# mLSTM, top-2 MoE and dense cosine layer on one core: conversions and preparations issued sooner, late weight low halves on VectorE, 128-row gathers for 64-slot tiles

## The chip, the cores and the metric

One Trainium2 chip, one of its cores. The metric is the device time of one execution in microseconds, taken as the median of repeated runs; lower is better.

## What is computed

Three layers follow one another, all in float32. Sizes: batch 2, 8 heads, 768 positions, head size 40, so 1536 tokens of 320 values; 8 experts of 320 x 1024 and 1024 x 320; a dense layer of 320 x 2048 and 2048 x 320.

```python
# 1. mLSTM: a gated recurrence per head, y[t] = sigmoid(o) * (C @ q) / max(|n . q|, 1)
C = f_stab * C + i_stab * outer(v_t, k_t); n = f_stab * n + i_stab * k_t
# 2. mixture of experts, two experts per token
noisy = x @ w_gate + log1p(exp(x @ w_noise)) * noise
top2 of noisy, softmax over the two
out[token] += weight * (relu(x @ w1[e]) @ w2[e])
# 3. dense layer
h = x @ w_in
out = (h * cos(h)) @ w_out
```

The kernel computes the mLSTM in chunks of 128 positions. Matrix products of layers 2 and 3 are made of float32r products of split operands: every operand is written as a high half (a rounded copy) and a low half (the operand minus the copy), and three products, high x high, high x low and low x high, are added.

## The kernel before, in words

The program is one core's, and the order of every engine's instructions is written out by hand. Five queues matter: PE (matmuls), ACT (ScalarE), DVE (VectorE), POOL (GpSimd) and SP (which issues plain DMAs). Each works strictly in the order in which the builder emits, and a function emitted in "step k" stands behind all that was emitted in steps before.

**Steps.** After the attention part come numbered steps k. Steps 0 to 79 are the expert layer: ten groups of eight steps. A group is one expert and a set of token slots; `groups` is: experts 0 and 1 with two slots (128 and 112 rows) for the first batch entry, experts 2 to 7 with four slots (128, 128, 128 and 64 rows) for both entries together, then experts 0 and 1 with two slots for the second entry. So groups 0, 1, 8 and 9 are narrow (240 columns) and groups 2 to 7 wide (448). Step 8g + f does slice f (128 of 1024 hidden values) of group g. From step 79 on the dense layer runs: `moe2_step(k - 79)`, 64 slices: four sets of 384 tokens by 16 slices of 128 hidden values.

**An expert step** (`expert_step`): first `split(k + 2)`, the weights of two steps ahead: ScalarE copies the raw slice (128 x 704) into `wh` (L597), and an engine subtracts to make the low half `wl` (L599), VectorE or POOL by a rule on k; then the first product `mm1` (eight matmuls, L606, into a PSUM tile `pS`); then ScalarE writes `relu` into the high part of `hb` (L658) and VectorE the low part (L661); then `flush`, which emits the second product of the step before (`mm2`, L611, L612, L615, for a fourth slot also L623, L624). The last matmuls of `mm2` (L615) need the low part of `hb`. `wh`, `wl` and three `pS` tiles rotate; at f = 7 the accumulators are copied out and stored (`fin1`).

**Gathers and preparation.** `gather(g, i)` fetches the rows of slot i of group g with an indirect DMA issued by POOL (L558); an index of an unused place is 0, which is a valid row. `prep_slot` transposes them in three matmuls (`prep_x`, L567), ScalarE copies them to `xh` (L569), VectorE makes the low part `xl` and a second part (L570, L572). They are put at steps by hand: those of group 2 at 13, 14, 15 and 15.

**Conversions.** The dense layer's weights come as float64 in 16 slices. `conv_load(f)` loads one, and `conv_ops(f)` gives five operations: three integer operations on VectorE that make a float32 (L726, L729, L733), ScalarE's high half (L736) and VectorE's low half (L739). `conv_sched(f, ks)` puts them at the five steps `ks`, and the load of slice f + 1 at the first of them. Slices 0 to 11 are done from step 18 on, one every 3.75 steps; 12 to 15 at steps written out, between 66 and 92. The results of slices 12 to 15 lie in a weight buffer of the experts.

**A dense slice** (`moe2_step`): `moe2_a`, the first product of 384 columns; `moe2_b`, reduction of the argument (ScalarE L755, VectorE L756, L757); two steps later `moe2_c`, sine and square on ScalarE (L768, L769) and the product with h on VectorE (L770), which frees the `pS` tile; `moe2_d`, the high half on ScalarE (L774) and the low half on POOL or VectorE (L776); and `moe2_e`, the second product. At step 80 the last `mm2` of the experts is flushed between slices 1 and 2.

**Combination.** `comb_gather` (L682) fetches a token's two expert outputs, `comb` (L689 on ScalarE, L691 on VectorE) adds them, `comb_t` prepares them as above. Those of the first 384 tokens stand at steps 66 to 77.

The order of the attention part and of the two routers isn't touched.

Of the kernel before, what the change touches and what calls it, by code (L numbers as in the profile page):

```python
# [9 lines left out]
FT = mybir.dt.float32  # L10
# [31 lines left out]
def tile_mlstm_moe_moe2(ctx, tc, qk, kv, og, gt, wcat, noise, wm1, wm2, cst, out):  # L42
# [304 lines left out]
    def cols(x, n, k):  # L347

        c0 = min(128 * k, DM - 128)
        return x[:n, c0:c0 + 128]  # L350
# [202 lines left out]
    def gather(g, i):  # L553
        d = GX.setdefault(g, {"xg": []})
        _, sz, j = groups[g]
        n = sz[i]
        t = mp.tile([128, DM], FT, name="xgt", tag="xg", bufs=6)
        G.indirect_dma_start(out=t[:n, :], out_offset=None, in_=XD[0:S, :] if g < 2 else XD[:, :],  # L558
                             in_offset=bass.IndirectOffsetOnAxis(ap=(idxe if g < 2 else idx)[:n, j + i:j + i + 1],
                                                                 axis=0))  # L560
        d["xg"].append(t)

    def prep_x(src, np_, xh, xl, n0, ps_=None):
        p = (ps_ or psM)()
        pv = p[:, :3 * np_].rearrange("p (k t) -> p k t", t=np_)
        for k in range(3):
            T.transpose(pv[:, k, :], cols(src, np_, k), ident[:np_, :np_])  # L567
        sl = slice(n0, n0 + np_)
        A.activation(xh[:, :, sl], pv, AF.Copy)  # L569
        V.tensor_tensor(out=xl[:, :, sl], in0=pv[:, 0:2, :], in1=xh[:, 0:2, sl].bitcast(FT), op=OP.subtract)  # L570

        V.tensor_tensor(out=xh[0:64, 2, sl], in0=pv[64:128, 2, :], in1=xh[64:128, 2, sl].bitcast(FT),  # L572
                        op=OP.subtract)
# [11 lines left out]
        prep_x(d["xg"][i], groups[g][1][i], d["xh"], d["xl"], 128 * i, ps_)  # L585

    SP = {}
    POOL_SPLIT = (1, 5, 7, 9, 65, 67, 75)

    def split(k):  # L590
        g, f = divmod(k, 8)
        if g >= NG:
            return
        raw = WB[groups[g][0]]
        wh = mp.tile([128, FW], FR, name="wh", tag="wh", bufs=4)
        wl = mp.tile([128, FW], FR, name="wl", tag="wl", bufs=4)
        A.activation(wh, raw[:, f, :], AF.Copy)  # L597
        eng = V if len(groups[g][1]) == 2 and (k % 2 and k not in POOL_SPLIT or k == 10) else G
        eng.tensor_tensor(out=wl, in0=raw[:, f, :], in1=wh.bitcast(FT), op=OP.subtract)  # L599
        SP[k] = (wh, wl)  # L600

    def mm1(p, n, wh, wl, xh, xl):
        ops = [(wh, 0, xh, 0), (wh, 1, xh, 1), (wl, 0, xh, 0), (wl, 1, xh, 1), (wh, 0, xl, 0), (wh, 1, xl, 1),
# [40 lines left out]
    def flush():  # L644
        if pend:
            pend.pop(0)()

    def expert_step(g, f):
        e, sz, _ = groups[g]
        d = GX[g]  # L650
        n = sum(sz)
        split(8 * g + f + 2)
        wh, wl = SP.pop(8 * g + f)
        p = psS()
        mm1(p, n, wh, wl, d["xh"], d["xl"])
        hb = new_h()
        hh, hl = hb[:, 0:448], hb[:, 512:896]
        A.activation(hh[:, :n], p[:, :n], AF.Relu)  # L658
        for a, z, o in ((0, min(n, 384), 512), (384, n, 448)):
            if a < n:  # L660
                V.scalar_tensor_tensor(out=hb[:, o:o + z - a], in0=p[:, a:z], scalar=0.0,  # L661
                                       in1=hh[:, a:z].bitcast(FT), op0=OP.max, op1=OP.subtract)
        flush()

        def st2():
            if f == 0:
                d["acc"] = [psA() for _ in sz]
            mm2(d["acc"], sz[:3], wh, wl, hh, hl, f == 0, f == 7)
            if len(sz) == 4:
                mm2h(d["acc"][3], wh, wl, hb, f == 0, f == 7)  # L670
            if f == 7:
                fin1(g)
        pend.append(st2)
# [27 lines left out]

    def conv_load(f):
        q = f // 4
        if f % 4 == 0:
            if q < 3:
                W2[q] = wp.tile([128, 2, 4, FW], FR, name=f"w2_{q}")
            else:
                W2[q] = big.tile([128, 2, 4, FW], FR, name="w2q", tag="W")
        raw = wp.tile([128, FW, 2], I32, name="raw2", bufs=2)
        Y.dma_start(raw, wm2[:, f, :].bitcast(I32).rearrange("p (w two) -> p w two", two=2))  # L710
        W2["raw", f] = raw

    def conv_ops(f):
        wh, wl = W2[f // 4][:, 0, f % 4, :], W2[f // 4][:, 1, f % 4, :]
        raw = W2["raw", f]
        lo, hi = raw[:, :, 0], raw[:, :, 1]
        def tmp(name, tag):
            if f < 13:
                return wp.tile([128, FW], I32, name=name, tag="ct", bufs=3)
            return mp.tile([128, FW], I32, name=name, tag=tag, bufs=4)  # L720

        t0 = tmp("c_t0", "wh")
        tt = {}

        def o1():
            V.tensor_scalar(t0, hi, 0x07FFFFFF, 3, op0=OP.bitwise_and, op1=OP.logical_shift_left)  # L726

        def o2():
            V.scalar_tensor_tensor(out=t0, in0=hi, scalar=-0x40000000, in1=t0, op0=OP.bitwise_and, op1=OP.bitwise_or)  # L729

        def o3():
            t1 = tt[0] = tmp("c_t1", "wl")
            V.scalar_tensor_tensor(out=t1, in0=lo, scalar=29, in1=t0, op0=OP.logical_shift_right, op1=OP.bitwise_or)  # L733

        def o4():
            A.activation(wh, tt[0].bitcast(FT), AF.Copy)  # L736

        def o5():
            V.tensor_tensor(out=wl, in0=tt[0].bitcast(FT), in1=wh.bitcast(FT), op=OP.subtract)  # L739
        return [o1, o2, o3, o4, o5]  # L740


# [60 lines left out]
    def moe2_step(k):  # L803
        if k < N2:
            moe2_a(k)
        if 2 <= k:
            moe2_c(k - 2)
        if k < N2:
            moe2_b(k)
        if 2 <= k:  # L810
            moe2_d(k - 2)
        if k < 3 or k in LATE:
            return
        if k < N2:
            moe2_e(k - 3 - sum(k > i for i in LATE))
        elif k == N2 + 1:
            for i in range(N2 - 3 - len(LATE), N2):
                moe2_e(i)
# [161 lines left out]
    put(12, router_a4, 1)  # L980
    for i in range(4):
        put(7 + i // 2, gather, 2, i)
        put((13, 14, 15, 15)[i], prep_slot, 2, i, (psA, psM)[i % 2])
    for g in range(2, NG - 1):
        n = len(groups[g + 1][1])
        for i in range(n):
# [5 lines left out]

    def conv_sched(f, ks):
        if f == 0:
            put(16, conv_load, 0)

        def first():
            o = conv_ops(f)
            o[0]()
            for k, op in zip(ks[1:], o[1:]):  # L1000
                put(k, op)
            if f + 1 < 16:
                put(ks[0], conv_load, f + 1)
        put(ks[0], first)

    K2 = 8 * NG
    for f in range(12):
        k = 18 + (15 * f) // 4
        conv_sched(f, (k, k + 1, k + 2, k + 2, k + 3))
    conv_sched(12, (66, 68, 69, 71, 71))  # L1010
    conv_sched(13, (78, 79, 80, 82, 83))
    conv_sched(14, (83, 84, 85, 88, 88))
    conv_sched(15, (87, 90, 91, 92, 92))
    for c in range(3):
        for k in range(2):
            put((66, 68, 71)[c] + k, comb_gather, 0, c, k)
# [163 lines left out]
```

## Time and profile before

| | us |
|---|---|
| median of 3 runs (lowest, highest) | 506.29 (506.05, 507.14) |
| the profiled execution | 505.76 |
| its span, first to last instruction | 504.0 |
| PE busy | 481.1 |
| VectorE, ScalarE, POOL busy | 353.2, 325.6, 273.1 |

All of these come from the profile page but the first. The span is 1.8 us shorter than the execution that it belongs to. Times in rows are microseconds from the start of the span. In a timeline a row is one instruction or several of one line merged; the number in brackets is the engine's idle time before it, and what ended it. Matmuls are pipelined, so the start of a matmul tells more than its end. TensorE's granted clock was 0.998 in the mean over the span.

### The profile page before, as it was taken

What the parts mean: (1) busy time and instruction counts of PE and PEld (TensorE: products, weight loads), DVE (VectorE), ACT (ScalarE), POOL (GpSimd) and SP (SyncE); (2) the same over time, 40 slices, a digit from 0 to 9 for tenths busy, and PEclk for the clock granted to TensorE, in tenths of its full rate; (3) what the DMA queues carried; (4) which work ended last, traced back from release to release, by engine and by line L of the source; (5) the groups of instructions that cost most, each with busy time, mean ns of one, the idle gap of its engine ahead of it and who ended that gap; (6) DMA issues with size and microseconds to landing.
All of it is one profiled execution on the core that took longest, in us unless ns stands there. A gap on an engine that the chain in (4) does not pass through costs nothing.

```text
span 504.0 us, 9162 instructions
## 1 busy us (share of the span) xinstructions
PE 481.1 (95%) x3295; PEld 466.0 (92%) x3295; DVE 353.2 (70%) x749; ACT 325.6 (65%) x691; POOL 273.1 (54%) x228
## 2 busy tenths in 40 slices
PE   5999889999999999999999989899999999999995
PEld 4998888989999999999999988899999999999995
DVE  4565697874577777787667588589756755787772
ACT  3787856655454545545553765678787787787772
POOL 4654665877558684968587786363364357200000
PEclk9999999999999999999999999999999999999999
DMA  6989754964739274645657373310020012001001
GB/s 200 299 286 295 236 180 144 322 211 152 294 128 322 103 260 176 257 182 188 257 166 263 117 284 100 105 52 1 0 92 29 0 35 84 2 2 39 1 2 45
DMA packets 25429, 74.47 MB, mean 148 GB/s; under 512 B 3840, under 2 KB 11456, under 8 KB 25376
## 3 DMA queue, kind: packets, MB, share of 16 engines
q1 hardware_dynamic: 22784, 65.20, 37.1%
q0 software_dynamic: 2592, 8.61, 5.7%
q8 instruction: 28, 0.46, 0.4%
q14 instruction: 25, 0.20, 0.1%
HBM read 64.57 MB, written 9.22 MB: 146 GB/s over the span
## 4 chain that ended last, share of the span: by engine, by line
PE 79%; DVE 9%; ACT 3%; issue 3%; DMA 2%; POOL 1%; SPq 1%; ACTq 0%; DVEq 0%; POOLq 0%
PE pS L606 34%; PE pA L615 10%; PE pA L611 10%; PE pA L612 10%; PE pS L321 3%; PE pM L567 2%; DMA wraw<-wm 2%; PE pA L262 1%; PE pA L623 1%; PE pA L624 1%; PE pS L317 1%; PE pM L366 1%; PE pA L253 1%; DVE c_t L729 1%; POOL xgt L558 1%
## 5 line engine op out<-in xcount | busy, mean ns | idle before, releaser
L599 POOL TENSOR_TENSOR wl<-wraw,wh 128x704 fp32r<-128x704 f32 x70 | 125.2, 1801 | 59.8 <-ACT wh L597 53.1
L661 DVE SCALAR_TENSOR_TENSOR hb<-pS,hb 128x384 fp32r<-128x384 f32 (+2 forms) x128 | 45.8, 390 | 45.2 <-ACT hb L658 44.5
L597 ACT ACTIVATE wh<-wraw 128x704 fp32r<-128x704 f32 x80 | 62.8, 786 | 15.8 <-PE pA L623 9.3
L606 PE MATMUL pS<-xh,wh 128*128 128x448 f32 (+1 forms) x240 | 69.3, 343 | 0.5 <-ACT xh L569 0.5
L606 PE MATMUL pS<-xh,w 128*128 128x384 f32 x288 | 66.3, 339 | 1.5 <-DVE m_t L770 1.5
L606 PE MATMUL pS<-xh,wl 128*128 128x448 f32 (+1 forms) x240 | 65.9, 329 | 1.0 <-POOL wl L599 1.0
L611 PE MATMUL pA<-wh,hb 128*128 128x320 f32 x208 | 62.3, 309 | 0.0
L612 PE MATMUL pA<-wl,hb 128*128 128x320 f32 x208 | 62.2, 309 | 0.0
L755 ACT ACTIVATE m_t<-pS,magic 128x384 f32<-128x384 f32 x64 | 37.1, 579 | 27.7 <-PE pS L606 27.2
L658 ACT ACTIVATE hb<-pS 128x448 fp32r<-128x448 f32 (+1 forms) x80 | 37.7, 471 | 26.7 <-PE pS L606 19.2
L606 PEld LDWEIGHTS pS<-xh,w 128*128 128x128 f32 x288 | 50.1, 189 | 2.9 <-DVE m_t L770 2.9
L770 DVE SCALAR_TENSOR_TENSOR m_t<-m_t,pS 128x384 f32<-128x384 f32 x64 | 35.4, 553 | 16.9 <-ACT m_t L769 16.3
L615 PE MATMUL pA<-wh,hb 128*128 128x320 f32 x208 | 44.0, 311 | 2.8 <-DVE hb L661 2.6
L606 PEld LDWEIGHTS pS<-xh,wl 128*128 128x128 f32 x240 | 42.8, 189 | 3.6 <-POOL wl L599 1.4
L606 PEld LDWEIGHTS pS<-xh,wh 128*128 128x128 f32 x240 | 40.5, 189 | 1.6 <-ACT xh L569 0.6
L776 POOL TENSOR_TENSOR wl<-m_t,wh 128x384 fp32r<-128x384 f32 x25 | 25.5, 1019 | 30.2 <-ACT wh L774 21.1
L756 DVE TENSOR_SCALAR m_t<-m_t 128x384 f32<-128x384 f32 x64 | 23.1, 361 | 26.4 <-ACT m_t L755 26.2
L606 PE MATMUL pS<-xl,wh 128*128 128x448 f32 (+1 forms) x160 | 39.6, 328 | 0.0
L611 PEld LDWEIGHTS pA<-wh,hb 128*128 128x128 f32 x208 | 38.7, 186 | 0.6
L612 PEld LDWEIGHTS pA<-wl,hb 128*128 128x128 f32 x208 | 38.7, 186 | 0.5
L569 ACT ACTIVATE xh<-pM 128x384 fp32r<-128x384 f32 (+2 forms) x38 | 17.6, 462 | 30.5 <-PE pM L567 30.4
L757 DVE SCALAR_TENSOR_TENSOR m_t<-pS,m_t 128x384 f32<-128x384 f32 x64 | 35.7, 557 | 2.2
(217 smaller groups left out, 1226.7 us busy)
## 6 DMA issues: line engine op xcount, KB each, us to landing
wraw<-wm SPq DMA_DIRECT2D x36, 704.0 KB
raw<-wm SPq DMA_DIRECT2D x16, 704.0 KB
gb<-gd SPq DMA_DIRECT2D x10, 512.0 KB
kv<-kv SPq DMA_DIRECT2D x12, 324.0 KB
qk<-qk SPq DMA_DIRECT2D x24, 160.0 KB
yd<-yt SPq DMA_DIRECT2D x22, 160.0 KB
wraw<-wm SPq DMA_DIRECT2D x8, 352.0 KB
ogt<-og SPq DMA_DIRECT2D x6, 320.0 KB
```

The costliest lines, as they stand in the source:

```text
L597: A.activation(wh, raw[:, f, :], AF.Copy)
L599: eng.tensor_tensor(out=wl, in0=raw[:, f, :], in1=wh.bitcast(FT), op=OP.subtract)
L606: T.matmul(p[:, :n], w[:, 128 * k:128 * k + 128], x[:, m, :], start=(i == 0), stop=(i == 7))
L611: T.matmul(a[:n, :DM], hh[:, s], wh[:, KW:], start=first, stop=False)
L612: T.matmul(a[:n, :DM], hh[:, s], wl[:, KW:], start=False, stop=False)
L615: T.matmul(a[:n, :DM], hl[:, s], wh[:, KW:], start=False, stop=last)
L658: A.activation(hh[:, :n], p[:, :n], AF.Relu)
L661: V.scalar_tensor_tensor(out=hb[:, o:o + z - a], in0=p[:, a:z], scalar=0.0, in1=hh[:, a:z].bitcast(FT), op0=OP.max, op1=OP.subtract)
L755: A.activation(t, m["p"], AF.Identity, bias=magic, scale=0.5 / PI)
L757: V.scalar_tensor_tensor(out=t, in0=m["p"], scalar=0.5 / PI, in1=t, op0=OP.mult, op1=OP.subtract)
L770: V.scalar_tensor_tensor(out=s, in0=s, scalar=1.0, in1=m["p"], op0=OP.subtract, op1=OP.mult)
L776: eng.tensor_tensor(out=m["hl"], in0=m["t"], in1=m["hh"].bitcast(FT), op=OP.subtract)
```

## The change

Seven edits:

- A gather of the fourth slot of a wide group fetches 128 rows instead of 64, and the transposes of a 64-slot tile are made with all 128 rows; the copies out of PSUM still take 64 columns.
- The rule of who makes a weight low half: VectorE for k in 3, 10, 11, 12, 13, 15 and for all k from 66 on, POOL for the rest. Before, VectorE had the odd k of narrow groups but 1, 5, 7, 9, 65, 67 and 75, and k = 10.
- From k = 66 on the low half is emitted after VectorE's low part of `hb` of the same step, not before it.
- Group 2's preparations stand at steps 12, 13, 14, 14.
- Conversions 0 to 11 begin at step 16 instead of 18, in the same rhythm, with the first load at step 14; conversion 12 joins that rhythm (61, 62, 63), its last two operations stay at 71; 13, 14 and 15 are put at other steps.
- The buffer for slices 12 to 15 is taken when it is first written (step 71) and not with the load.
- Slice 0's sine, square and product are emitted at step 80 behind slice 1's reduction, ahead of the flush and of what else stands at that step, instead of at step 81.

```diff
     def gather(g, i):
-        n = sz[i]
+        n = sz[i] if i < 3 else 128
...
     def prep_x(src, np_, xh, xl, n0, ps_=None):
         p = (ps_ or psM)()
-        pv = p[:, :3 * np_].rearrange("p (k t) -> p k t", t=np_)
+        m = 128 if np_ == 64 else np_
+        pv = p[:, :3 * m].rearrange("p (k t) -> p k t", t=m)
         for k in range(3):
-            T.transpose(pv[:, k, :], cols(src, np_, k), ident[:np_, :np_])
+            T.transpose(pv[:, k, :], cols(src, m, k), ident[:m, :m])
+        pv = pv[:, :, :np_]
...
-    POOL_SPLIT = (1, 5, 7, 9, 65, 67, 75)
+    V_SPLIT = (3, 10, 11, 12, 13, 15)
...
         A.activation(wh, raw[:, f, :], AF.Copy)
-        eng = V if len(groups[g][1]) == 2 and (k % 2 and k not in POOL_SPLIT or k == 10) else G
-        eng.tensor_tensor(out=wl, in0=raw[:, f, :], in1=wh.bitcast(FT), op=OP.subtract)
         SP[k] = (wh, wl)
+        eng = V if k in V_SPLIT or k >= 66 else G
+
+        def low():
+            eng.tensor_tensor(out=wl, in0=raw[:, f, :], in1=wh.bitcast(FT), op=OP.subtract)
+
+        if k >= 66:
+            return low
+        low()
...
-        split(8 * g + f + 2)
+        low = split(8 * g + f + 2)
...
                                        in1=hh[:, a:z].bitcast(FT), op0=OP.max, op1=OP.subtract)
+        if low:
+            low()
         flush()
...
         q = f // 4
-        if f % 4 == 0:
-            if q < 3:
-                W2[q] = wp.tile([128, 2, 4, FW], FR, name=f"w2_{q}")
-            else:
-                W2[q] = big.tile([128, 2, 4, FW], FR, name="w2q", tag="W")
+        if f % 4 == 0 and q < 3:
+            W2[q] = wp.tile([128, 2, 4, FW], FR, name=f"w2_{q}")
...
         def o4():
-            A.activation(wh, tt[0].bitcast(FT), AF.Copy)
+            if f == 12:
+                W2[3] = big.tile([128, 2, 4, FW], FR, name="w2q", tag="W")
+            A.activation(part(0), tt[0].bitcast(FT), AF.Copy)
...
     def moe2_step(k):
         if k < N2:
             moe2_a(k)
-        if 2 <= k:
+        if 3 <= k:
             moe2_c(k - 2)
         if k < N2:
             moe2_b(k)
+        if k == 1:
+            moe2_c(0)
         if 2 <= k:
             moe2_d(k - 2)
...
-        put((13, 14, 15, 15)[i], prep_slot, 2, i, (psA, psM)[i % 2])
+        put((12, 13, 14, 14)[i], prep_slot, 2, i, (psA, psM)[i % 2])
...
-            put(16, conv_load, 0)
+            put(14, conv_load, 0)
...
-    for f in range(12):
-        k = 18 + (15 * f) // 4
-        conv_sched(f, (k, k + 1, k + 2, k + 2, k + 3))
-    conv_sched(12, (66, 68, 69, 71, 71))
-    conv_sched(13, (78, 79, 80, 82, 83))
-    conv_sched(14, (83, 84, 85, 88, 88))
-    conv_sched(15, (87, 90, 91, 92, 92))
+    for f in range(13):
+        k = 16 + (15 * f) // 4
+        conv_sched(f, (k, k + 1, k + 2, k + 2, k + 3) if f < 12 else (k, k + 1, k + 2, 71, 71))
+    conv_sched(13, (77, 78, 78, 81, 81))
+    conv_sched(14, (82, 83, 84, 85, 88))
+    conv_sched(15, (85, 86, 87, 88, 90))
```

`part(i)` is the tile slice that was named `wh` (i = 0) and `wl` (i = 1) in `conv_ops` before.

## Rows read from the trace of the kernel before

**Rows 1.** The page, part 1: busy time, share of the span, instructions.

```profile
PE 481.1 (95%) x3295; PEld 466.0 (92%) x3295; DVE 353.2 (70%) x749; ACT 325.6 (65%) x691; POOL 273.1 (54%) x228
```

**Rows 2.** Stretches: from:to and length, busy us per engine (instructions), PEclk, DMA share, GB/s.

```profile
200.00:210.00 10.00, 10.00 (x61) 9.68 (x60) 7.60 (x14) 6.18 (x12) 8.82 (x6) 1.00 0.44 149
...
281.27:316.23 34.96, 31.95 (x246) 30.89 (x245) 26.79 (x45) 21.91 (x43) 25.98 (x17) 1.00 0.51 183
316.23:361.01 44.78, 42.63 (x263) 41.14 (x261) 37.20 (x70) 34.14 (x68) 19.39 (x18) 1.00 0.14 42
108.81:121.48 12.67, 11.55 (x85) 10.78 (x83) 7.71 (x19) 7.19 (x15) 8.42 (x6) 1.00 0.59 220
```

**Rows 3.** Timeline of PE, 280 to 362 us: start, length, instruction, idle before.

```profile
283.78 0.39 PE L606 MATMUL pS<-xh,wh 128*128 128x240 f32 x2
...
285.56 0.39 PE L606 MATMUL pS<-xh,wh 128*128 128x240 f32 x2
...
298.81 0.56 PE L615 MATMUL pA<-wh,hb 128*128 128x320 f32 x2 [1.72 <-DVE hb L661]
...
322.76 0.97 PE L606 MATMUL pS<-xh,w 128*128 128x384 f32 x4 [1.31 <-DVE m_t L770]
...
325.57 0.85 PE L606 MATMUL pS<-xh,w 128*128 128x384 f32 x4
...
328.27 0.85 PE L606 MATMUL pS<-xh,w 128*128 128x384 f32 x4
...
355.17 0.96 PE L606 MATMUL pS<-xh,w2q 128*128 128x384 f32 x4 [0.60 <-DVE m_t L770]
```

**Rows 4.** Timeline of PE, 155 to 177 us: last matmul of each four-slot step.

```profile
161.91 0.31 PE L624 MATMUL pA<-wl,hb 128*128 128x320 f32 x1
...
165.47 0.31 PE L624 MATMUL pA<-wl,hb 128*128 128x320 f32 x1
...
169.02 0.31 PE L624 MATMUL pA<-wl,hb 128*128 128x320 f32 x1
...
172.79 0.31 PE L624 MATMUL pA<-wl,hb 128*128 128x320 f32 x1
...
176.01 0.31 PE L624 MATMUL pA<-wl,hb 128*128 128x320 f32 x1
```

**Rows 5.** Timeline of PE, 96 to 124 us: its two waits.

```profile
109.84 0.49 PE L606 MATMUL pS<-xh,wl 128*128 128x240 f32 x2 [0.65 <-POOL wl L599]
...
118.81 0.67 PE L606 MATMUL pS<-xh,wh 128*128 128x448 f32 x2 [0.47 <-ACT xh L569]
```

**Rows 6.** Timeline of POOL, rows of 85 to 160 and 270 to 362 us.

```profile
108.10 4.01 POOL L599 TENSOR_TENSOR wl<-wraw,wh 128x704 fp32r<-128x704 f32 x2
...
288.92 1.08 POOL L682 DMA_INDIRECT yg<-yd,r_pos  x1
...
295.84 1.72 POOL L599 TENSOR_TENSOR wl<-wraw,wh 128x704 fp32r<-128x704 f32 x1
```

**Rows 7.** Timeline of DVE, 276 to 362 us.

```profile
289.07 0.88 DVE L599 TENSOR_TENSOR wl<-wraw,wh 128x704 fp32r<-128x704 f32 x1
...
295.60 2.72 DVE L733 SCALAR_TENSOR_TENSOR c_t<-raw,c_t 128x704 int32<-128x704 int32 x1
...
321.36 0.88 DVE L733 SCALAR_TENSOR_TENSOR c_t<-raw,c_t 128x704 int32<-128x704 int32 x1
```

**Rows 8.** Groups of DVE, 281.27 to 316.23; the last row 316.23 to 361.01.

```profile
L599 DVE TENSOR_TENSOR wl<-wraw,wh 128x704 fp32r<-128x704 f32 x5 | 5.0, 1002 | 0.4 <-ACT wh L597 0.4
L691 DVE SCALAR_TENSOR_TENSOR xt<-yg,r_w 128x320 f32<-128x320 f32 x3 | 4.1, 1351 | 0.1
...
L726 DVE TENSOR_SCALAR c_t<-raw 128x704 int32<-128x704 int32 x2 | 2.3, 1136 | 0.0
...
L691 DVE SCALAR_TENSOR_TENSOR xt<-yg,r_w 128x320 f32<-128x320 f32 x3 | 1.6, 547 | 0.0
```

**Rows 9.** The chain that ended last, in order of time: start, length, what.

```profile
369.27 1.39 PE pS L606 x8
```

More of the change, by code (lines that the diff above doesn't have):

```diff
@@ L713, in conv_ops, with part @@
     def conv_ops(f):
-        wh, wl = W2[f // 4][:, 0, f % 4, :], W2[f // 4][:, 1, f % 4, :]
         raw = W2["raw", f]
         lo, hi = raw[:, :, 0], raw[:, :, 1]
+        def part(i):
+            return W2[f // 4][:, i, f % 4, :]
         def tmp(name, tag):
@@ L735, in o4 @@
         def o4():
-            A.activation(wh, tt[0].bitcast(FT), AF.Copy)
+            if f == 12:
+                W2[3] = big.tile([128, 2, 4, FW], FR, name="w2q", tag="W")
+            A.activation(part(0), tt[0].bitcast(FT), AF.Copy)
         def o5():
-            V.tensor_tensor(out=wl, in0=tt[0].bitcast(FT), in1=wh.bitcast(FT), op=OP.subtract)
+            V.tensor_tensor(out=part(1), in0=tt[0].bitcast(FT), in1=part(0).bitcast(FT), op=OP.subtract)
         return [o1, o2, o3, o4, o5]
```

## The prediction

> **What bounds the kernel now.** The page comes first: PE is busy for 481.1 of 504.0 us [rows 1], so time can only be won where PE stands still or does needless work. The busy time of each engine in stretches then says where that is. A stretch in the middle of the expert layer (200 to 210 us) has PE busy for all 10 us, with DVE at 7.60 [rows 2]; there the time is the number of matrix columns, and a shorter VectorE, ScalarE or DMA gains nothing. Three stretches are not like that [rows 2]: steps 12 to 16 (108.81 to 121.48), steps 64 to 79, the last two experts (281.27 to 316.23), and the first 16 slices of the dense layer (316.23 to 361.01). Last, the timeline of PE gives the step that the columns alone would take: 1.78 us for a two-slot expert (283.78 to 285.56) [rows 3], 3.22 for a four-slot one (172.79 to 176.01) [rows 4], 2.70 for a slice of the dense layer (325.57 to 328.27) [rows 3]. What a stretch takes beyond that is the most that can be won in it. I count by the spacing of starts and not by PE's busy time, because a matmul that waits in the middle still counts as busy.
>
> The engines work their queues in order, so a late VectorE instruction is found by asking what stands ahead of it.
>
> **Steps 12 to 16: earlier preparation, low half 12 on VectorE.** The stretch lasts 12.67 us. Its columns: four steps of 1.78 (7.12), step 16 with 1.61 (half of a 3.22 step) and 0.88 (the second half of a 1.78 step), and four slot preparations. Such a preparation adds 3.56 - 3.22 = 0.34 (161.91 to 165.47 against 172.79 to 176.01) [rows 4], four of them 1.36. The sum is 10.97, so 1.70 us are lost. They are lost at two places [rows 5]: PE waits at 109.84 for POOL's low half, and at 118.81 for ScalarE's copy of the last slot. POOL is late because split 12 is queued behind the four gathers, and it starts only at 108.10 [rows 6]. The change gives split 12 to VectorE, where it is one more 0.88 instruction (289.07) [rows 7] in a stretch in which DVE is busy for 7.71 of 12.67 us, and issues all four preparations by step 14, so that step 15 (1.78) lies over the last copy and its two subtractions. What is late next is POOL's split 14; it has two steps and an idle POOL. Bounds: nothing, if another wait comes out right behind, and 1.70; I take **1.7**, since after the change neither place has a queue ahead of it.
>
> **128-row gathers and transposes.** The fourth slot of a four-slot expert has 64 rows. The interval with its three transposes is 3.77 (169.02 to 172.79) [rows 4], with a 128-row slot 3.56, although the 64-row one has half the columns. So the small shape costs 0.21 more, and the change makes it a 128-row one. It stands in five groups where PE is full (groups 3 to 7; the group of steps 12 to 16 is in the sum above): 5 x 0.21 = **1.05**. The bounds are 0 and 1.05. The gather on POOL moves 64 more rows; POOL has been waiting for its weights there, and the fourth gather is needed three steps after its issue, so I cost it at nothing. The copies out read the same 64 columns as before.
>
> **Conversions two steps sooner (steps 16 to 63).** The same five operations on the same engines. Their loads go out two steps sooner, the first at step 14 instead of 16; each stands ahead of at most one more weight chunk of the same size on SP's queue, and a chunk is due some five steps after its issue, over 15 us. If VectorE is late with a buffer, SP waits there and the chunks wait behind it, inside those five steps. PE's full stretch covers them (DVE 7.60 of 10 us [rows 2]), before and after: nothing. If that cover went, the price would be that of the third operation held ahead of h, below.
>
> **Steps 64 to 79.** Columns: 2.51 for step 64 (281.27 to 283.78; its second half is still a four-slot one) [rows 2, 3], 15 x 1.78 = 26.70, and five preparations x 0.34 = 1.70; the sum is 30.91 against 34.96, so **4.05** are lost. The longest wait is PE's at 298.81 (1.72) for hb, the low half of h [rows 3]. VectorE had been in one instruction: the third operation of conversion 12, at 295.60 for 2.72 us [rows 7]. The same operation takes 0.88 elsewhere (321.36) [rows 7]; the long one runs beside POOL's weight subtraction at 295.84 [rows 6]. So a VectorE instruction that reads and writes SBUF is held until POOL's subtraction ends; the three combinations of this stretch, 1.35 us each where the next three take 0.55 [rows 8], say the same. The change takes the held work away: three operations of conversion 12 go to steps 61 to 63, where PE is full, the weight subtractions of steps 64 to 77 go from POOL to VectorE, and there they stand behind h.
>
> VectorE's account for the stretch: 26.79 busy [rows 2], plus nine more low halves x 0.88 = 7.9, minus conversion 12's three operations (2.7 for the third, 0.9 unheld for the second, and 1.8 of the 2.3 that the two first operations took, conversion 13's own, unheld, being taken at 0.5: 5.4), plus two operations of conversion 13 (1.8), minus the hold in the combinations (4.1 - 1.6 = 2.5) and in the five low halves it has already (5.0 - 5 x 0.88 = 0.6) [rows 7, 8]: 28.0 of 30.9 us. It fits, but steps 71 to 77 are the tight ones, with a combination or a preparation beside each low half. A low half of step k is due two steps after its issue and h nearly two products later, so a lag of half a step is harmless. Bounds: 0 and 4.05; I take **3.9**, close to the upper end, since all named causes go.
>
> **Dense layer, first 16 slices.** Columns: three first products of 1.39 [rows 9] and 0.88 of the experts' last second product for the slices 0 to 2, 13 x 2.70, three preparations x 0.34: 41.2 against 44.78 [rows 2], so 3.6 are lost. About 1.4 of it is the wait at 322.76 (1.31 idle) for the last VectorE step of slice 0, and 0.8 the one at 355.17 (0.60 idle) [rows 3]; the rest, 1.4, lies in small pieces between. Ahead of slice 0 stood conversion 13's third operation at 321.36 (0.88) [rows 7]; it goes to step 78, and slice 0's sine is issued a step sooner, ahead of the copies out of the last expert. That gives 1.4. Conversion 15's late operations, behind the second wait, go to steps 86 to 90: 0.8. Against this, conversion 13's last two now stand in step 81, a ScalarE copy and a VectorE subtraction, ahead of slice 1's sine and its last step. One operation of that size is 0.88 [rows 7]; I take 0.8 for the pair, as one of them lies beside other work. Conversions 14 and 15 fill steps 82 to 88, one operation in each; two more such steps with a third of a microsecond each make 0.6. Net: **0.8** (from -1.5, if every moved operation stalls PE for most of its length, to 3.6).
>
> **Sum.** 1.7 + 1.05 + 3.9 + 0.8 = 7.45. The profiled execution took 505.76 (span 504.0), 0.53 below the median of 506.29; so 498.3 for that one, **498.8** as a median.
>
> **A rule against it.** POOL's gathers at 288.92 (1.08) ran beside VectorE's subtraction at 289.07, which took its plain 0.88 [rows 6, 7]. The Trainium skill (GPSIMD Engine Reference, 8. Key points) says that GpSimd shares its SBUF interfaces with VectorE and contends with instructions that have two SBUF inputs; it makes no exception for gathers. By that rule, the trace agrees for subtractions and not for gathers.
>
> **The rivals.**
> (a) The dense layer gives back more than it gets: the closer-packed conversions cost PE 1.5 instead of a gain of 0.8. For it speaks that each of steps 82 to 88 now has a conversion operation; against it that the same number of operations was there before. 498.8 + 2.3 = 501.1. Chance 0.17.
> (b) Gathers hold VectorE as subtractions do. Six combination gathers at 1.08 [rows 6] add 6.5 to VectorE's 28.0 and make it 34.5, so VectorE bounds steps 64 to 79 and 3.4 of the 3.9 are not won: 502.2. Against it stands the row at 289.07. Chance 0.1.
> (c) The 128-row shape does not remove the 0.21, because the cost belongs to the slot's place and not to its rows: 499.85. Against it: the 128-row slots one step sooner do not have it. Chance 0.08.
> (d) Slower: each of the 14 low halves on VectorE takes what it takes on POOL, 1.8, because something holds it. VectorE's account is then 28.0 + 14 x 0.92 = 40.9, and steps 64 to 79 take 5.9 more than now; with 3.55 won elsewhere, 508.6. It decides from about 1.63 per low half on, where the account is 38.5 and eats those 3.55 too. For it: VectorE was held for as long at 295.60. Against it: what held it, POOL's subtraction, leaves the stretch. Chance 0.04.
>
> **The numbers.** The forecast, within 1.2 us of 498.8, has 0.58; the remaining 0.03 are for mishaps of either sign. The lower end of the range is where steps 64 to 79 win all 4.05 and the dense layer has its 2.2 without the new stalls, and half a microsecond of its small pieces too: 1.7 + 1.05 + 4.05 + 2.7 = 9.5, so 496.8 (all bounds together, 10.4, would give 495.9). The upper end takes in (a), (c) and (b): 502.4. A measurement of this kernel tells about 0.2% from no change, 1.0 us; all cases but (d) and mishaps lie past it: faster 0.94, same 0.03, slower 0.03.
>
> **What would show it.** Right: in steps 12 to 16 no PE wait on POOL; the interval with the fourth slot 3.56; steps 64 to 79 near 31 us with no wait for hb, VectorE's low halves at 0.88 and no weight subtraction on POOL; a wait of well under 1.3 us at the dense layer's fourth slice. Wrong: VectorE low halves over 1.2 us in that stretch, a PE wait for wl from VectorE, or PE idle for m_t over 2 us in the first 16 slices.

## The result, and the profile after

| | before | after |
|---|---|---|
| median of 4 runs (lowest, highest), us | 506.72 (506.05, 507.14) | 499.48 (499.09, 500.10) |
| the profiled execution | 505.76 | 499.09 |
| its span | 504.0 | 497.4 |

The ratio is 0.9857, 95% interval 0.9839 to 0.9876: faster by 7.2 us, where 7.5 was predicted. 499.48 lies 0.7 above the 498.8 of the forecast and inside its range.

The stages are cut at the starts of matmuls: step 12's first product, step 17's, step 64's, the dense layer's first and its 17th slice's. For the changed kernel the busy times by stretch (columns as in [rows 2]; steps 12 to 16, steps 64 to 79, 16 dense slices) are:

```profile
109.24:120.24 11.00, 11.00 (x85) 10.84 (x83) 6.28 (x19) 7.08 (x15) 6.39 (x4) 1.00 0.89 317
278.92:309.79 30.87, 30.87 (x246) 30.84 (x245) 27.60 (x53) 21.52 (x43) 8.11 (x7) 1.00 0.52 184
309.79:353.78 43.99, 42.87 (x262) 41.14 (x261) 38.13 (x69) 33.82 (x68) 19.30 (x18) 1.00 0.14 43
```

| stage, us | predicted gain | before | after | gain |
|---|---|---|---|---|
| steps 12 to 16 | 1.7 | 12.67 | 11.00 | 1.67 |
| steps 17 to 63 (128-row shape) | 1.05 | 159.79 | 158.68 | 1.11 |
| steps 64 to 79 | 3.9 | 34.96 | 30.87 | 4.09 |
| dense layer, first 16 slices | 0.8 | 44.78 | 43.99 | 0.79 |

The four gains make 7.66. The two spans differ by 6.6, because in this profile step 12 starts 0.43 later and the last 48 slices take 0.63 more (143.62 against 142.99). The change touches next to nothing there: two more profiles of versions with the same last 48 slices show 143.07 and 143.66, and step 12 starts anywhere from 108.69 to 110.70. So I compare stages within profiles, and medians for the whole.

The page's busy line answers to [rows 1]; PE has lost 2.5 us of busy time and POOL 19:

```profile
PE 478.6 (96%) x3295; PEld 466.2 (94%) x3295; DVE 355.5 (71%) x759; ACT 325.1 (65%) x691; POOL 254.1 (51%) x218
```

**Steps 64 to 79.** The timeline of DVE after, then its groups from 278.92 to 309.79, then the timeline of POOL, answer to [rows 6 to 8]:

```profile
290.87 0.88 DVE L604 TENSOR_TENSOR wl<-wraw,wh 128x704 fp32r<-128x704 f32 x1
...
316.75 1.14 DVE L751 TENSOR_TENSOR w2q<-c_t,w2q 128x704 fp32r<-128x704 f32 x1
317.81 0.54 DVE L782 SCALAR_TENSOR_TENSOR m_t<-m_t,pS 128x384 f32<-128x384 f32 x1
```
```profile
L604 DVE TENSOR_TENSOR wl<-wraw,wh 128x704 fp32r<-128x704 f32 x14 | 12.3, 881 | 0.0
...
L701 DVE SCALAR_TENSOR_TENSOR xt<-yg,r_w 128x320 f32<-128x320 f32 x3 | 1.6, 550 | 0.1
```
```profile
290.60 0.95 POOL L692 DMA_INDIRECT yg<-yd,r_pos  x1 [0.30 <-issue]
```

The low halves are 14, at 881 ns in the mean; the combinations have fallen from 1351 to 550 ns in the mean; PE is busy for the whole stretch. A gather on POOL at 290.60 runs beside VectorE's low half at 290.87, which takes its plain 0.88.

**128-row shape and dense layer.** The timeline of PE after: the last matmuls of three four-slot steps, as in [rows 4]; then the first products of the dense layer's third and fifth slices and PE's two other waits there, as in [rows 3].

```profile
167.52 0.31 PE L632 MATMUL pA<-wl,hb 128*128 128x320 f32 x1
171.07 0.31 PE L632 MATMUL pA<-wl,hb 128*128 128x320 f32 x1
174.29 0.31 PE L632 MATMUL pA<-wl,hb 128*128 128x320 f32 x1
...
313.46 0.86 PE L614 MATMUL pS<-xh,w 128*128 128x384 f32 x4
...
318.41 0.95 PE L614 MATMUL pS<-xh,w 128*128 128x384 f32 x4 [0.48 <-DVE m_t L782]
...
327.10 0.96 PE L614 MATMUL pS<-xh,w 128*128 128x384 f32 x4 [0.29 <-DVE m_t L782]
...
336.14 0.96 PE L614 MATMUL pS<-xh,w 128*128 128x384 f32 x4 [0.35 <-DVE m_t L782]
```

The interval that holds the 64-slot tile's transposes (167.52 to 171.07) is 3.55, like that of a 128-row slot; before it was 3.77. Where the 0.22 lay is told by the timeline of PE before, at the transposes of a 128-row slot and of the 64-row one, each with the product behind it:

```profile
165.61 0.49 PE L567 MATMUL pM<-ci,xgt 128*128 128x128 f32 x3
165.86 0.66 PE L606 MATMUL pS<-xh,wh 128*128 128x448 f32 x2
...
169.26 0.40 PE L567 MATMUL pM<-ci,xgt 64*128 64x64 f32 x3
169.58 0.68 PE L606 MATMUL pS<-xh,wh 128*128 128x448 f32 x2
```

From the start of the last matmul ahead (165.47 and 169.02 [rows 4]) to the transposes it is 0.14 and 0.24, and from there to the product 0.25 and 0.32: 0.17 of the 0.22 stands at the two ends of the small group, though its transposes have half the columns.

The waits of 1.31 and 0.60 [rows 3] are gone; three smaller ones stand in their place. The one at 318.41 is the fifth slice's, for the tile that slice 1 frees, and its cause is in the DVE rows above: slice 1's last VectorE step, at 317.81, stood behind conversion 13's low half.

### The profile page after: what moved, and what is told of

Same layout as the page of the kernel before. It is cut to its first block, busy times and chain, and to the rows that moved or that the text cites. A ratio compares the mean times of both kernels' runs of the same rounds, so it can differ in the third digit from the quotient of the medians.

```text
span 497.4 us, 9151 instructions
## 1 busy us (share of the span) xinstructions
PE 478.6 (96%) x3295; PEld 466.2 (94%) x3295; DVE 355.5 (71%) x759; ACT 325.1 (65%) x691; POOL 254.1 (51%) x218
## 4 chain that ended last, share of the span: by engine, by line
PE 85%; DVE 9%; ACT 3%; issue 1%; DMA 1%; POOL 0%; SPq 0%; ACTq 0%; POOLq 0%
PE pS L614 37%; PE pA L623 11%; PE pA L619 11%; PE pA L620 11%; PE pS L321 3%; PE pM L568 2%; PE pA L262 2%; PE pM L366 1%; PE pA L631 1%; PE pA L632 1%; PE pS L317 1%; PE pA L253 1%; DVE r_am L497 1%; DMA qk<-qk 1%; DVE ppt L271 1%
## 5 line engine op out<-in xcount | busy, mean ns | idle before, releaser
L604 POOL TENSOR_TENSOR wl<-wraw,wh 128x704 fp32r<-128x704 f32 x60 | 106.5, 1788 | 52.5 <-ACT wh L599 49.0
L558 POOL DMA_INDIRECT xgt<-xd,idx x28 | 34.0, 1215 | 5.2 <-issue 3.0
```

## The experiments

Each kernel is compared with the kernel before on the same chip (506.67 beside experiments 1, 3, 4 and 5, 506.64 beside 6 to 9, 506.2 beside 2, 10, 11 and 12). My theory is the prediction's, stage by stage; the rivals are in the expectations. The edits are shown as diffs against the changed kernel where nothing else is said.

**1. POOL makes the late low halves again.**

```diff
-        eng = V if k in V_SPLIT or k >= 66 else G
+        eng = V if k in V_SPLIT or (k >= 66 and k % 2 and k not in (67, 75)) else G
...
-        if k >= 66:
-            return low
```

> The changed kernel, but the weight low halves of k >= 66 are shared between POOL and VectorE by the old rule and stand ahead of h, as before; conversion 12 stays moved. Theory (POOL's subtractions hold VectorE, and that is the loss of steps 64 to 79): the stretch goes back from 30.9 to 34 to 35 us, with VectorE operations of 1.5 to 2.9 us beside POOL's and PE waits for hb and for wl; 503 to 504 us in all. Rival (conversion 12's operations ahead of h were the loss, and they are gone): the stretch stays at or under 32 us, 499.5 to 500.6.

502.78 us, ratio 0.9918 (0.9902 to 0.9935). Steps 64 to 79 take 34.62, nearly the 34.96 of before, although conversion 12's three operations are issued at steps 61 to 63 here too; the last of them starts at 282.14, over 20 us ahead of PE's long wait below. First the stretch, then the timelines of DVE, POOL and PE:

```profile
281.00:315.62 34.62, 31.92 (x246) 30.97 (x245) 27.86 (x44) 21.82 (x43) 23.64 (x16) 1.00 0.48 164
```
```profile
296.83 2.60 DVE L604 TENSOR_TENSOR wl<-wraw,wh 128x704 fp32r<-128x704 f32 x1 [0.51 <-ACT wh L599]
...
299.68 2.69 DVE L699 SCALAR_TENSOR_TENSOR xt<-yg,r_w 128x320 f32<-128x320 f32 x1
```
```profile
296.96 1.72 POOL L604 TENSOR_TENSOR wl<-wraw,wh 128x704 fp32r<-128x704 f32 x1
```
```profile
303.54 0.56 PE L621 MATMUL pA<-wh,hb 128*128 128x320 f32 x2 [1.47 <-DVE hb L667]
```

Other VectorE instructions are now the long ones: a low half takes 2.60 beside POOL's subtraction at 296.96 (0.88 in the changed kernel) and a combination 2.69 (0.55 there). The wait for hb is back.

**2. The late low halves alone**, on the kernel before. The edit takes only this part of the change, so conversion 12 stays at steps 66, 68 and 69:

```diff
-        eng = V if len(groups[g][1]) == 2 and (k % 2 and k not in POOL_SPLIT or k == 10) else G
-        eng.tensor_tensor(out=wl, in0=raw[:, f, :], in1=wh.bitcast(FT), op=OP.subtract)
         SP[k] = (wh, wl)
+        eng = V if k >= 66 or len(groups[g][1]) == 2 and (k % 2 and k not in POOL_SPLIT or k == 10) else G
...
+        if k >= 66:
+            return low
...
+        if low:
+            low()
         flush()
```

> The kernel before with one part of the change alone: the low halves of k from 66 on go to VectorE, behind h. Theory (POOL's subtractions are what held VectorE in steps 64 to 79, and nearly all of the gain there is theirs): although conversion 12 stays at steps 66, 68 and 69, its third operation falls from 2.72 to 0.88 us, steps 64 to 79 take 31.0 to 32.0 us against 34.96 before, the wait for hb is gone, and the time is 3.0 to 3.9 us under before: 502.8 to 503.7. Rival (conversion 12's operations are a cause of their own, as the prediction booked 3.6 us of VectorE's account for them): with them left in the stretch VectorE's account is 30.7 of 30.9 us, it becomes the bound there, and steps 64 to 79 take 33 us or more: 504.7 or more.

503.07 us, ratio 0.9942 (0.9922 to 0.9962). Stretches (steps 64 to 79, then the 16 dense slices), then the timeline of DVE:

```profile
281.40:312.94 31.54, 31.42 (x247) 30.92 (x246) 27.59 (x54) 21.64 (x43) 10.59 (x8) 1.00 0.56 203
312.94:357.72 44.78, 42.62 (x263) 41.14 (x261) 37.22 (x70) 34.13 (x68) 19.42 (x18) 1.00 0.14 42
```
```profile
295.60 0.89 DVE L741 SCALAR_TENSOR_TENSOR c_t<-raw,c_t 128x704 int32<-128x704 int32 x1
```

Conversion 12's third operation, in the same place, falls from 2.72 [rows 7] to 0.89. With experiment 1 this settles the stretch: the subtractions leaving POOL (to stand behind h on VectorE) are worth 3.42 of the 4.09 alone, and without that the rest gives 0.34. My sum had taken 5.4 us off VectorE's account for conversion 12's leaving. Here it stays, and its three operations take 2.3 (0.55, 0.89 and 0.89) where they took 5.5 before (1.76, 1.02 and 2.72): 3.2 of it was hold, which goes with POOL's subtractions wherever conversion 12 stands. The account of the stretch, 27.59, is no higher than the changed kernel's 27.60. The dense layer gains nothing from this part (44.78, as before).

**3. Conversions 12 to 15 at their old steps.**

```diff
-        conv_sched(f, (k, k + 1, k + 2, k + 2, k + 3) if f < 12 else (k, k + 1, k + 2, 71, 71))
-    conv_sched(13, (77, 78, 78, 81, 81))
-    conv_sched(14, (82, 83, 84, 85, 88))
-    conv_sched(15, (85, 86, 87, 88, 90))
+        conv_sched(f, (k, k + 1, k + 2, k + 2, k + 3) if f < 12 else (66, 68, 69, 71, 71))
+    conv_sched(13, (78, 79, 80, 82, 83))
+    conv_sched(14, (83, 84, 85, 88, 88))
+    conv_sched(15, (87, 90, 91, 92, 92))
```

> The changed kernel with conversions 12 to 15 at their old steps (66, 68, 69, 71, 71 and so on); low halves on VectorE behind h. Theory (the hold by POOL is the loss): conversion 12's three operations now take 0.5 to 0.9 us each, steps 64 to 79 take 30.9 to 31.5, and the first 16 dense slices 43.5 to 45; 499.5 to 500.5 in all. Rival (the operations themselves ahead of h are the loss): steps 64 to 79 take 33 to 35 with a PE wait for hb over 1 us; 502 to 504.

499.53 us, ratio 0.9858 (0.9841 to 0.9874). Steps 64 to 79 take 31.51, the dense slices 44.23: moving the four conversions is worth 0.64 and 0.24 in the stages, nothing that the median can tell.

**4. The low half ahead of h again.**

```diff
-        if k >= 66:
-            return low
         low()
```

> The changed kernel, with VectorE's low halves of k >= 66 emitted ahead of the low part of h instead of behind it. Theory (h has over 1 us of slack and the low half is 0.88): steps 64 to 79 stay within 0.3 us of 30.9; 499.3 to 499.9. Rival (the order is what protects PE): PE waits for hb again, 1 us or more in the stretch; 500.5 to 502.

499.67 us, ratio 0.9867 (0.9851 to 0.9883). Steps 64 to 79 take 31.21 against 30.87: the order is worth 0.34. PE's list has no wait for hb, so the rival falls.

**5. 64-row gathers and transposes again.**

```diff
-        n = sz[i] if i < 3 else 128
+        n = sz[i]
...
-        m = 128 if np_ == 64 else np_
+        m = np_
```

> The changed kernel with 64-row gathers and transposes of the fourth slot again. Theory (the small shape costs 0.21 us each): the five intervals with it are 3.77 again instead of 3.56, 1.05 us in steps 17 to 63, and 0.1 to 0.2 in steps 12 to 16; 500.5 to 500.9. Rival (the place costs, not the shape): no interval differs from the changed kernel's; 499.3 to 499.7.

500.66 us, ratio 0.9887 (0.987 to 0.9903). Steps 17 to 63 take 159.76, 1.08 more. The timeline of PE shows the 3.77 of [rows 4] again (168.63 to 172.40), in a kernel that is otherwise the changed one:

```profile
168.63 0.31 PE L632 MATMUL pA<-wl,hb 128*128 128x320 f32 x1
172.40 0.31 PE L632 MATMUL pA<-wl,hb 128*128 128x320 f32 x1
```

So the 0.22 belongs to the 64-row shape and not to the slot's place; rival (c) falls. Gathers and transposes went back together here; that the transposes are what costs PE is read from the rows of PE above.

**6. Slice 0's sine a step later again.**

```diff
-        if 3 <= k:
+        if 2 <= k:
             moe2_c(k - 2)
...
-        if k == 1:
-            moe2_c(0)
```

> The changed kernel with slice 0's sine, square and product at step 81 again. Theory (the gain of the dense layer's start comes from conversion 13's third operation being gone, and what the sine wins at slice 3 is lost at slice 4 anyway): a PE wait of 0.5 to 0.8 us at slice 3 and a smaller one at slice 4, the first 16 slices at 43.8 to 44.3 us against 43.99; 499.3 to 499.9 in all. Rival (the sine's place is worth what I booked for it): the first 16 slices take 44.6 to 45.4; 500.1 to 501.

500.03 us, ratio 0.9874 (0.9846 to 0.9903). The 16 slices take 43.91 against 43.99: beside the moved conversions the sine's new place is worth nothing. In the timeline of PE the wait has only changed its slice, from the fifth to the fourth:

```profile
316.38 0.96 PE L614 MATMUL pS<-xh,w 128*128 128x384 f32 x4 [0.54 <-DVE m_t L782]
```

**7. The early steps as before.**

```diff
-    V_SPLIT = (3, 10, 11, 12, 13, 15)
+    V_SPLIT = (3, 10, 11, 13, 15)
...
-        put((12, 13, 14, 14)[i], prep_slot, 2, i, (psA, psM)[i % 2])
+        put((13, 14, 15, 15)[i], prep_slot, 2, i, (psA, psM)[i % 2])
```

> The changed kernel with low half 12 on POOL and group 2's preparations at steps 13, 14, 15, 15, as before. Theory: both waits of steps 12 to 16 come back (for wl at step 12, for xh at step 16), steps 12 to 16 take 12.5 to 12.7 us instead of 11.00; 501.0 to 501.4. Rival (128-row transposes and the earlier conversion load have their part in it): 11.5 to 12.2; 500 to 500.7.

502.53 us, ratio 0.9913 (0.9893 to 0.9933). Steps 12 to 16 take 12.71. The waits of PE (total us, times, longest) are those of [rows 5]:

```profile
PE pS L614 <- POOL wl L604: 0.7, 1, 0.7
...
PE pS L614 <- ACT xh L571: 0.5, 1, 0.5
```

The edit has two parts, the place of low half 12 and that of the preparations; they were not tried apart. Each has one of the two waits.

**8 and 9. The last conversions spread out.** What the prediction booked against the change (0.8 for conversion 13 in step 81, 0.6 for the close packing) should come back when the operations stand where no sine is waited for.

```diff
-    conv_sched(13, (77, 78, 78, 81, 81))
-    conv_sched(14, (82, 83, 84, 85, 88))
-    conv_sched(15, (85, 86, 87, 88, 90))
+    conv_sched(13, (77, 77, 78, 83, 83))
+    conv_sched(14, (79, 80, 85, 87, 88))
+    conv_sched(15, (86, 87, 90, 92, 92))
```

> The changed kernel with conversions 13, 14, 15 at (77, 77, 78, 83, 83), (79, 80, 85, 87, 88) and (86, 87, 90, 92, 92): two operations of conversion 14 in the pause of VectorE while the dense layer starts, and steps free of operations between. Theory (what is left in the first 16 slices is conversion operations ahead of the product that frees the PSUM tile): 41.3 to 42.5 us for them instead of 43.99; 497.3 to 498.3. Rival (it is the length of the chain ScalarE, VectorE, PE itself, whatever the operations): 43.5 to 44.2; 499 to 499.8.

The second one puts all of conversion 13 ahead of the dense layer: 13 at (77, 77, 78, 78, 78), 14 at (79, 80, 83, 86, 88), 15 at (85, 86, 90, 92, 92).

> As the run before it, with conversion 13 finished at step 78 (77, 77, 78, 78, 78), (79, 80, 83, 86, 88) and (85, 86, 90, 92, 92). Theory: 41.2 to 42.3 us for the first 16 slices and no more than 0.3 us more in steps 64 to 79; 497.2 to 498.2. Rival (the last expert steps have no room on VectorE for two more operations): steps 64 to 79 take 31.5 to 32.5; 498.5 to 499.5.

498.65 us, ratio 0.9832 (0.9812 to 0.9851), and 499.4, ratio 0.984 (0.9817 to 0.9864). The 16 slices take 42.05 and 41.78, both as the theory has them, and PE's list of waits for m_t is empty.

The medians are not as expected: those of experiments 6 to 9 lie above their theories' ranges (by 0.1, 1.1, 0.35 and 1.2). All four profiles have steps 64 to 79 at 32.25 to 32.44, 1.4 more than the changed kernel's first profile. That would cover the excess if the other executions have it too, which no run tells; the last section comes back to it. For experiment 9, its 32.39 lies in the range of its rival (no room for two more operations), but experiments 6 to 8 without those two show as much, so the rival is not borne out.

**10 and 11. The spread version and the changed kernel once more, on one chip.**

> e7_spread unchanged, once more and on one chip with the changed kernel. Theory (conversions 13, 14 and 15 in the changed kernel stand ahead of sines that PE waits for; spread out they do not): the first 16 dense slices take 41.8 to 42.2 us against 43.9 to 44.0, and the time is 1.3 to 2.0 us under the changed kernel's. Rival (the first 16 slices give back what they win, elsewhere): within 0.5 us of the changed kernel.

> The changed kernel once more, on one chip with the three others. Theory (the changed kernel's stages are as in its first profile): steps 64 to 79 in 30.9 us, the first 16 dense slices in 43.9 to 44.0, and the time is 499.0 to 500.0, 6.6 to 7.4 under before. Rival (the pause of 1.4 us that stood in steps 70 to 73 in the profiles of e5 to e8 belongs to these kernels and not to one chip): it is here too, with 32.3 in steps 64 to 79.

497.76 us (496.64 to 498.39), ratio 0.9828 (0.9809 to 0.9847), against 498.76 (497.82 to 499.63), ratio 0.9848 (0.983 to 0.9867), five runs each. The stretches of the spread version, steps 64 to 79 and 16 dense slices:

```profile
279.51:310.39 30.88, 30.88 (x247) 30.85 (x246) 27.62 (x53) 21.54 (x43) 8.15 (x7) 1.00 0.52 183
310.39:352.44 42.05, 42.05 (x262) 41.11 (x261) 36.84 (x69) 33.73 (x68) 19.21 (x18) 1.00 0.15 45
```

The stage is 1.94 shorter in both profiles; the medians differ by 1.0, less than expected, and their intervals overlap. The stage gain is shown, the gain of the whole is not firmly so. The changed kernel's second median, 498.76, lies a little under the 499.0 to 500.0 expected; against before it is 7.4 less, the most that was expected.

These two runs show something that the first profile did not. The timeline of PE of the changed kernel's second profile, steps 12 to 16:

```profile
115.75 0.52 PE L568 MATMUL pM<-ci,xgt 128*128 128x128 f32 x3 [0.36 <-DMA xgt<-xd,idx]
```

PE waits for the last gather of group 2, whose preparation the change has put a step earlier. POOL's instruction for it stands at 107.10, and PE goes on at 115.75, more than 8 us later. Steps 12 to 16 take 11.49 there (11.56 in the spread version, with a wait of 0.42). Experiment 1's profile has the same wait with 0.80, 8 and 9 with 0.24 and 0.20; in the changed kernel's first profile it is not there.

This gather is the fourth, which the change also made 128 rows. The view of its DMA ends with the time from issue to landing in us, first for the changed kernel's second profile (128 rows), then for experiment 5 (64 rows):

```profile
xgt<-xd,idx POOLq DMA_INDIRECT x1, 8.5
```
```profile
xgt<-xd,idx POOLq DMA_INDIRECT x1, 7.3
```

In the ten profiles that tell it, 64 rows land in 6.7 to 7.3 us (before, experiments 2 and 5) and 128 rows in 7.8 to 8.9 (seven others). Experiment 5, with 64 rows and the early preparation, has no such wait, and neither has experiment 7, with 128 rows and the old preparation. That is one profile each, and of the ten with both parts only five list the wait; so it is likely, not shown, that it takes both.

**12. POOL's low halves of the first dense slices go to VectorE**, on top of the spread version.

```diff
-        eng = V if k != "g" and k >= 41 else G
+        eng = V if k != "g" and (k < 14 or k >= 41) else G
```

> As e7_spread (the last three conversions at other steps), and the low halves of the first 14 dense slices go from POOL to VectorE too. Theory (moving a subtraction off POOL gains only where VectorE has room and PE waits for it; in the first 16 dense slices of e7_spread PE has no wait left, and VectorE is busy for some 38 of 42 us): 14 x 0.55 = 7.7 us go onto VectorE, some 3 come back because its conversion operations (1.32 and 1.35 us there against 0.88) are no longer held, and VectorE's account comes to about 43 us: the first 16 slices take 42.3 to 43.5 us, and the time is 0.2 to 1.5 above e7_spread. Rival (what POOL holds on VectorE is also what is left here): 41.4 us, 0.6 under e7_spread.

497.72 us, ratio 0.984 (0.9814 to 0.9866). The stretch takes 42.09, as without it: neither the theory's loss nor the rival's gain. First its row, then two groups of DVE in it:

```profile
309.97:352.06 42.09, 42.09 (x262) 41.11 (x261) 37.95 (x82) 33.81 (x68) 0.00 (x0) 1.00 0.08 26
```
```profile
L751 DVE TENSOR_TENSOR w2q<-c_t,w2q 128x704 fp32r<-128x704 f32 x3 | 2.7, 888 | 0.0
L743 DVE SCALAR_TENSOR_TENSOR c_t<-raw,c_t 128x704 int32<-128x704 int32 x3 | 2.7, 884 | 0.0
```

VectorE has 13 instructions more in the stretch (82 against 69), 7.1 us of low halves, yet its busy time grows by only 1.1 (36.84 to 37.95). My 43 was wrong: 6.0 us came back, not 3. In the spread version the same two groups read 1349 and 1321 ns. POOL's 13.4 us of subtractions there (13 of 1.03 us) had cost VectorE nearly half their length.

## Why the prediction was right, and where its steps were not

- **Steps 12 to 16, 1.7.** 1.67 measured, and experiment 7 gives the 1.7 back. One sentence of the step failed: "What is late next is POOL's split 14". What is late next is the fourth gather, by 0 to 0.8 us from profile to profile. I had counted the copies and subtractions that move forward with the preparation, but not how long the gather in front of it needs to land; and that 64 more rows make it land later, I had costed at nothing.
- **128-row shape, 1.05.** 1.11 measured, 1.08 by experiment 5: five times 0.22.
- **Steps 64 to 79, 3.9.** 4.09 measured, a shade past the bound of 4.05 worked out from columns. The mechanism stands by experiments 1 and 2. Every low half beside a gather keeps its 0.88, so rival (b) falls; rival (d) falls with the 881 ns. The VectorE account came to 27.60 where 28.0 was forecast, but two of its readings were off. The three combinations did not take 1.35 us each: 1351 ns is the mean of two plain ones (0.54 and 0.55) and a long one, by the timeline of DVE before:

```profile
304.59 2.96 DVE L691 SCALAR_TENSOR_TENSOR xt<-yg,r_w 128x320 f32<-128x320 f32 x1
```

  And of the 5.4 for conversion 12's leaving, 3.2 was hold (experiment 2), and not all of it left. Its second operation, now issued at step 62, is held there in turn, by two subtractions of POOL, and its third runs inside the stretch (from 278.92). The timelines of DVE and POOL after:

```profile
275.52 4.02 DVE L739 SCALAR_TENSOR_TENSOR c_t<-raw,c_t 128x704 int32<-128x704 int32 x1
...
280.06 0.88 DVE L743 SCALAR_TENSOR_TENSOR c_t<-raw,c_t 128x704 int32<-128x704 int32 x1
```
```profile
275.39 3.39 POOL L604 TENSOR_TENSOR wl<-wraw,wh 128x704 fp32r<-128x704 f32 x2
```

  PE lists no wait there, so this hold, the longest of VectorE's in the changed kernel's trace, costs nothing that shows.

  The rule of the Trainium skill (GPSIMD Engine Reference, 8. Key points) is that GpSimd contends with VectorE instructions of two SBUF inputs. The traces agree for POOL's subtractions (0.88 becomes 2.60 in experiment 1) and not for its gathers (0.88 stays 0.88).
- **Dense layer, 0.8.** 0.79 measured, and that it came so near is in part luck. Booked as won were 1.4 and 0.8; the spread version wins 2.73, as much as the lower end of the range had with 0.5 of small pieces (2.7). Booked against it were 0.8 for the pair in step 81 and 0.6 for the close packing; what spreading gets back is 1.94. From the third to the fifth slice's first product the changed kernel takes 4.95 (313.46 to 318.41); the spread version takes 4.40, by the timeline of PE of experiment 10:

```profile
314.05 0.86 PE L614 MATMUL pS<-xh,w 128*128 128x384 f32 x4
...
318.45 0.85 PE L614 MATMUL pS<-xh,w 128*128 128x384 f32 x4
```

  So 0.55 of the 1.94 stood at the pair and 1.39 in the slices behind it: the pair was booked somewhat too high, the close packing at less than half. An error of 0.5 in what is won and one of 0.5 in what is lost cancel. Rival (a) falls, as the layer gains.
- **The share of the sine within the 1.4 was wrong.** The step named conversion 13's leaving and the sine's earlier issue together. With the conversions at their new steps the sine's place is worth nothing (43.91 without it and 43.99 with it). With the old ones the slices take 44.23, against 44.78 in experiment 2, where sine and conversions are both old; so there it may be worth up to 0.55. The two parts work on the same wait, 1.31 at the fourth slice: with the sine alone (experiment 3) none is listed there, with the conversions alone (experiment 6) 0.54 is left. In the changed kernel the sine's gain there is lost again at the fifth slice (0.48).

The median's 0.7 above the forecast is no step of the sum. The stages gave 7.66 for the 7.45 booked, the medians 7.24; how late step 12 starts and how long the last slices take varies by more than that between profiles, and the kernel before had 506.72 here, 0.43 over the median that the forecast started from.

## What to carry to other kernels

Before you move work from one engine to another, look at how long the other engine's instructions take while it runs: a move of 13 subtractions from POOL cost VectorE 1.1 us of busy time instead of 7.1, because it had been paying for them already. Move it where PE waits for VectorE (3.4 us here), and expect nothing where it doesn't. A preparation that is issued a step sooner may need its gather a step sooner too (no run here tried it); and among moved operations, place with most care those behind which a waited-for step stands.

## What the runs showed of the hardware that was not expected

- A VectorE instruction with one SBUF input lengthens beside POOL's subtractions too. The first operation of a conversion, in the groups of DVE of the 16 dense slices, in the changed kernel and in experiment 12, where POOL has none:

```profile
L736 DVE TENSOR_SCALAR c_t<-raw 128x704 int32<-128x704 int32 x2 | 2.6, 1296 | 0.0
```
```profile
L736 DVE TENSOR_SCALAR c_t<-raw 128x704 int32<-128x704 int32 x2 | 1.0, 519 | 0.0
```

  The Trainium skill's section named above (GPSIMD Engine Reference, 8. Key points) lists VectorE instructions in a 2-port performance mode beside those with two inputs; whether this one runs in such a mode no run here shows.

- The hold goes both ways. In the timelines of DVE and POOL before, a conversion's low half keeps its 0.88, and the subtraction beside it takes 2.38 instead of the usual 1.72:

```profile
300.25 0.88 DVE L739 TENSOR_TENSOR w2q<-c_t,w2q 128x704 fp32r<-128x704 f32 x1
```
```profile
300.33 2.38 POOL L599 TENSOR_TENSOR wl<-wraw,wh 128x704 fp32r<-128x704 f32 x1 [1.18 <-issue]
```

  The recorded starts do not tell which of the two is held: here VectorE starts 0.08 ahead of POOL, and at 295.60 [rows 6, 7] 0.24 ahead, where it was the one held.
- VectorE's product with h, which has one input in PSUM, is not lengthened: in the 16 dense slices its 14 instances take 547 ns in the mean with POOL's 13 subtractions there (experiment 10) and 550 without (experiment 12).
- A 64-row transpose group between 128-row matmuls costs 0.22 us more than the 128-row one with twice the columns. The Trainium skill (TensorEngine Tiling (Array Packing), Key Properties) says that a change of tiling mode drains TensorE; that would give such a cost, but no run here shows that a drain is what takes the 0.22.
- The profiles of experiments 6 to 9, all from one chip, have steps 64 to 79 at 32.25 to 32.44 where every other profile with the late low halves behind h, and all else new, has 30.87 or 30.88. The loss is spread over steps 71 to 73: their first products start 2.30, 2.12 and 2.47 us apart in experiment 6, against 1.77, 1.78 and 2.04 in the changed kernel's first profile. VectorE's h there comes after an idle time that no wait explains, by the timeline of DVE of experiment 6:

```profile
293.50 0.41 DVE L669 SCALAR_TENSOR_TENSOR hb<-pS,hb 128x240 fp32r<-128x240 f32 x1 [1.44 <-issue]
```

  The kernel of experiment 8 was profiled again as experiment 10, on another chip, and had 30.88; the changed kernel, in experiment 11 on that chip, had 30.88 too. So the loss is not the kernel's. The granted clock is 1.00 in it. Its cause stays open.
